# A list-scheduled transformer kernel: other queues and gates for the early stores, and products of constants ahead of the first weights

## The chip, the cores and the metric

The kernel runs on one core of a Trainium2 chip. The metric is the device time of one execution in microseconds (us). "TensorE" (PE in the profile; PEld is its weight load) multiplies matrices into eight banks of the accumulator memory; "VectorE" (DVE), "ScalarE" (ACT) and "GpSimd" (POOL) work on elements; "SyncE" (SP) here only issues transfers. SPq and ACTq in the profile are the queues on which SyncE and ScalarE issue transfers.

## The reference

Two blocks with residuals over 2048 tokens of 640 values. The first is attention over segments of 32 tokens; eight memory rows, which are outputs of the segment before, stand ahead of each segment, so the 64 segments depend on each other in a chain.

```python
x = A_x
h = x + _A_ref(_layernorm(x), A_mem0, A_Wq, A_Wk, A_Wv, A_Wo, A_seg_len)   # 32 heads of 128
h2 = h + _B_ref(_layernorm(h), B_W_gate, B_W_up, B_W_down)

# _A_ref, for each segment s of 32 tokens:
h = concatenate([mem, xs])                       # 8 memory rows + 32 tokens
q, k, v = h @ Wq, h @ Wk, h @ Wv
p = softmax(where(mask, q k^T * scale, -1e9))
o = (p v) @ Wo
mem = o[:8]; outs.append(o[8:])

# _B_ref:
h = (gate * (gate > 0)) * up                     # gate = x @ W_gate, up = x @ W_up, 1728 columns
return h @ W_down
```

## The kernel before

**Work.** A segment has 40 rows. 32 of them, the eight memory rows and the first 24 tokens, go through the chain of segments; the last eight tokens of each segment (the "rest") do not depend on the memory, so their query, key and value rows are made ahead for four segments at once. There are 16 such sets q of 128 rest rows, and each has six parts: query and key for either half of the heads (`p` = 0, 1) and values for either half (`p` = 2). A part is `groups`: five chunks of the contraction, each four products of 32 columns of rows by 512 columns of weights in one bank. `spread` evicts a query or key part, transposes it on VectorE into a staging tile `stg` (keys are reordered by GpSimd as well) and stores it to the scratch tensor `scr_qk` (line 1584); `values` evicts a value part into `stg` and stores it to `scr_v` (line 1601). `load_rs` brings the rest rows of one segment back into `RS`.

**The first 90 us.** The first nine sets (`EARLY = 9`) are made while the weights arrive: Wq, Wk and Wv in ten pieces each, then Wo in eight pieces of four heads. The rest rows of sets 0 to 3 and 4 to 7 come by `ln1r(0)` and `ln1r(1)`: a load of 128 rows (names "ldxr" and "ldxr1"), a layer norm on VectorE and ScalarE, a transpose by TensorE (20 products with the identity) and an eviction into `xr`. `ln1(0)` loads the first segments' rows ("ldx"). Rest rows of later sets are transposed by a transfer (line 1509). For sets 0 to 7 the names begin with "e": their `scr_qk` stores are issued by ScalarE, their `scr_v` stores by SyncE, and the latter wait until the fourth piece of Wo, `("Wo", 12)`, has landed. The early sets have up to eight banks and more staging tiles than later ones.

**A segment.** `main_qk` and `main_v` make query, key and value rows of the 32 rows; `scores` has the mask's seed, the products, an exponential on ScalarE, the sum by products with `bones`, logarithm and exponential for the reciprocal, and a product on VectorE; `pv` weights the values; `wo_early` and `wo` multiply by Wo (lines 1996 and 2015), `wo_add` adds the halves; `mem_next` copies the new memory rows into the next segment's input and transposes them (lines 1665 and 1668), which starts the next segment. Parts of rest sets, `rest_o` and the gate and up projections (`ahead`) are put into the segments as further work for TensorE. After the last segment come the weights of the second block and the down products.

**What sets the order.** All steps are declared by `op` with the engine, what they read and write, the buffers that they take, a cost and a transfer channel. `_Sched.schedule` then lists them once, in Python, with those costs: of the steps that are ready it takes the one with the highest level, which is the longest path to the end plus `BIAS[name]` and `BIAS["name@segment"]`. The result is a fixed order of instructions on each engine; at run time each engine works through its list and waits on semaphores. An eviction declared by `either` goes to ScalarE or VectorE, as `ENGINE` says, or else as the list comes out. `chan=(name, n)` allows n transfers of that name at a time. A transfer holds up whatever stands behind it in its engine's list until its inputs are there.

Two products of constants (`ones`, line 1866) fill banks 6 and 7 once at the start.

## Time and profile before

| | us |
|---|---|
| median of 3 runs | 998.73 (997.84 to 1000.79) |
| time of the profiled execution | 999.62 |
| span of the profiled execution | 997.5 |
| TensorE busy | 973.1 (98% of the span) |
| VectorE busy | 600.3 |
| ScalarE busy | 517.1 |
| GpSimd busy | 112.6 |

The span is measured from the first to the last instruction of the profile; the time of the execution is 2.1 us longer. The busy time of TensorE counts a matmul from its start to its modelled end, and matmuls overlap, so that it also holds time in which they run slowly. Rows of a group give its count, its busy time and the mean of one in ns, then the idle time just before them and what ended it.

### The profile page before, as it was taken

How to read it: one execution, taken by the hardware profiler on the slowest of the kernel's cores; microseconds unless marked ns; L12 is line 12 of the kernel's file. 1: busy time of each engine (PE TensorE's matmuls, PEld its weight loads, DVE VectorE, ACT ScalarE, POOL GpSimd, SP SyncE). 2: the span in 40 equal slices, each digit the busy share in tenths (PEclk: the TensorE clock that was granted, in tenths of full speed). 3: DMA queues.
4: the chain of work that ended last, by engine and by line, in shares of the span. 5: the costliest groups of instructions: out<-in, count | busy, mean ns of one | idle time of the engine just before them, and what ended most of it. 6: DMA issues, size and time to landing. Idle time of an engine off the chain costs nothing.

```text
span 997.5 us, 54364 instructions
## 1 busy us (share of the span) xinstructions
PE 973.1 (98%) x25380; PEld 528.0 (53%) x24412; DVE 600.3 (60%) x1307; ACT 517.1 (52%) x1264; POOL 112.6 (11%) x264
## 2 busy tenths in 40 slices
PE   6998999999999999999999999999999999999998
PEld 2344555555555555555565556555555556543343
DVE  5834666767675767566666676666665756523332
ACT  2245566566565565566555565556554665631020
POOL 3341011111011011001000010000100000100000
PEclk9999999999999999999999999999999999999999
DMA  9995121223131333232222343333233353289211
GB/s 334 407 334 137 44 57 55 68 67 76 35 90 40 85 74 79 53 80 65 72 77 61 86 105 85 86 88 78 55 79 82 76 92 85 53 270 288 76 40 40
DMA packets 181552, 103.60 MB, mean 104 GB/s; under 512 B 126212, under 2 KB 177484, under 8 KB 181324
## 3 DMA queue, kind: packets, MB, share of 16 engines
q1 hardware_dynamic: 175948, 95.51, 34.4%
q10 hardware_dynamic: 5376, 4.63, 1.4%
q8 instruction: 195, 3.19, 1.3%
q14 instruction: 33, 0.27, 0.1%
HBM read 67.30 MB, written 29.75 MB: 97 GB/s over the span
## 4 chain that ended last, share of the span: by engine, by line
PE 87%; SPq 3%; DMA 1%; ACTq 1%; ACT 1%; DVE 1%; issue 1%; POOL 0%; DVEq 0%
PE ps L1554 47%; PE ps L1996 7%; PE ps L2015 7%; PE ps L1719 7%; PE ps L1811 4%; PE ps L1638 3%; PE ps L1755 3%; PE ps L1962 3%; PE ps L1532 2%; PE ps L1937 2%; PE ps L1923 1%; SPq L2133 1%; ACTq L1598 1%; DMA scr_o<-osr 1%; SPq L1792 1%; SPq L2149 1%
## 5 line engine op out<-in xcount | busy, mean ns | idle before, releaser
L1388 ACT ACTIVATE tok<-ps 128x512 bf16<-128x512 f32 x225 | 133.4, 597 | 124.0 <-PE ps L1554 116.8
L1554 PE MATMUL ps<-Wk,xT 128*32 128x512 bf16 x2560 | 180.7, 379 | 0.6 <-ACT tok L1388 0.4
L1554 PE MATMUL ps<-Wv,xT 128*32 128x512 bf16 x2560 | 176.3, 379 | 0.0
L1554 PE MATMUL ps<-Wq,xT 128*32 128x512 bf16 x2560 | 169.3, 379 | 0.5 <-DVE xT L1668 0.3
L2045 DVE STREAM_TRANSPOSE QT<-tok 128x512 bf16<-128x512 bf16 x128 | 90.5, 708 | 50.7 <-ACT tok L1388 48.7
L2045 DVE STREAM_TRANSPOSE KT<-tok 128x512 bf16<-128x512 bf16 x128 | 90.8, 709 | 32.6 <-ACT tok L1388 31.4
L1554 PEld LDWEIGHTS ps<-Wq,xT 128*32 128x32 bf16 x2560 | 69.1, 97 | 68.4 <-DVE xT L1668 9.0
L1554 PEld LDWEIGHTS ps<-Wk,xT 128*32 128x32 bf16 x2560 | 65.9, 96 | 56.4 <-DVE xT L1668 3.9
L1932 ACT ACTIVATE E<-ps 128x224 bf16<-128x224 f32 x128 | 45.7, 357 | 91.6 <-PE ps L1927 88.0
L1389 DVE CAST oT<-ps 128x320 bf16<-128x320 f32 x128 | 56.8, 485 | 47.8 <-PE ps L1967 38.7
L2015 PE MATMUL ps<-Wo,oT 128*32 128x160 bf16 x4096 | 83.2, 233 | 0.3
L2015 PEld LDWEIGHTS ps<-Wo,oT 128*32 128x32 bf16 x4096 | 74.5, 97 | 14.5 <-ACT oT L1388 3.6
L1996 PE MATMUL ps<-Wo,oT 128*32 128x320 bf16 x2048 | 81.2, 300 | 0.8 <-ACT Vm L1388 0.6
L1554 PEld LDWEIGHTS ps<-Wv,xT 128*32 128x32 bf16 x2560 | 60.7, 96 | 38.4 <-DVE tok L1389 0.4
L1909 POOL COPY QT<-RS 128x256 bf16<-128x256 bf16 x64 | 25.8, 403 | 472.0 <-PE ps L1927 471.8
L1388 ACT ACTIVATE Vm<-ps 128x512 bf16<-128x512 f32 x121 | 71.5, 591 | 11.9 <-PE ps L1554 6.5
L1665 DVE CAST_PREDICATED xm<-turn,ps 128x64 bf16<-128x64 uint16 x126 | 28.0, 222 | 69.5 <-PE ps L1532 69.4
L1389 DVE CAST tok<-ps 128x512 bf16<-128x512 f32 x95 | 62.5, 658 | 9.9 <-PE ps L1554 9.8
L1996 PEld LDWEIGHTS ps<-Wo,oT 128*32 128x32 bf16 x2048 | 52.7, 96 | 27.7 <-DVE oT L1389 8.1
L1980 POOL COPY oTr<-oT 128x128 bf16<-128x128 bf16 x128 | 41.1, 321 | 198.6 <-ACT oT L1388 109.3
L1388 ACT ACTIVATE ps<-seed 128x384 f32<-128x384 bf16 x128 | 59.2, 489 | 1.4 <-DVE half L2004 1.3
L2004 DVE TENSOR_TENSOR half<-ps,half 128x320 bf16<-128x320 f32 x64 | 31.5, 492 | 42.2 <-ACT half L1388 41.8
(102 smaller groups left out, 1456.1 us busy)
## 6 DMA issues: line engine op xcount, KB each, us to landing
RS<-scr_qk SPq DMA_DIRECT2D x63, 128.0 KB, 2.3
big<-in_A_x_dram SPq DMA_DIRECT2D x34, 160.0 KB, 2.7
Wq<-in_A_Wq_dram SPq DMA_DIRECT2D x10, 512.0 KB, 7.1
Wk<-in_A_Wk_dram SPq DMA_DIRECT2D x10, 512.0 KB, 8.7
Wv<-in_A_Wv_dram SPq DMA_DIRECT2D x10, 512.0 KB, 7.7
Wo<-in_A_Wo_dram SPq DMA_DIRECT2D x8, 640.0 KB, 11.1
Wgs<-in_B_W_gate_dram SPq DMA_DIRECT2D x30, 160.0 KB, 3.0
Wus<-in_B_W_up_dram SPq DMA_DIRECT2D x30, 160.0 KB, 2.9
```

The source lines that it names most:

```text
L1388: return e.activation(dst, src, ACTF.Copy)
L1389: return e.tensor_copy(dst, src)
L1554: o = pe.matmul(out, lhs[c], rhs, start=(c == 0), stop=(c == DC - 1), skip_group_check=True)
L1638: o = pe.matmul(bank(bk)[p0:p0 + 32, 0:2 * SLICE], oTr[b][:, h, :], cols(h, 2 * a, 2 * a + 2), start=(h < 2), stop=(h >= H - 2), skip_grou ...
L1719: o = pe.matmul(bank(bk)[32 * i:32 * i + 32, 0:512], wt[:, c, 32 * i:32 * i + 32], xn2T[0][:, :, c * 128:(c + 1) * 128], start=(c == 0), s ...
L1811: pe.matmul(bank(ba)[:, 0:512], lhs, Wd[:, j, 0:512], start=(j == 0), stop=(j == FC - 1), skip_group_check=True)
L1932: op("act", lambda a: a.activation(E[:, g, :, 0:56], sco(BS[g]), ACTF.Exp, scale=SCALE), r=["table"], w=[("E", g)], x=[BS[g]], dur=0.36, n ...
L1980: op("pool", lambda e: e.tensor_copy(oTr[ob][:, 16 * g:16 * g + 16, XR * y:XR * y + XR], oT[:, 16 * g:16 * g + 16, 0:XR]), r=[("oT", g, 0) ...
L1996: o = pe.matmul(bank(BA)[p0:p0 + 32, 0:2 * SLICE], oT[:, h, XR:40], cols(h, 2 * b2, 2 * b2 + 2), start=(i == 0 and jj < 2), stop=(i == 3 a ...
L2004: op("dve", lambda v: v.tensor_tensor(half[1][:, :], bank(BA)[:, 0:2 * SLICE], half[0][:, :], ALU.subtract), r=["half0"], w=["half1"], x=[ ...
L2015: o = pe.matmul(bank(BW)[32 * j:32 * j + 32, 0:SLICE], oT[:, 16 + 4 * jj + i, XR:40], cols(h, j, j + 1), start=(i == 0 and jj == 0), stop= ...
L2045: op("dve", lambda v, tb=tb, dst=dst: v.transpose(dst, tok[tb.at][:, :].rearrange("p (h r) -> p h r", r=32)), w=[("QT" if p == 0 else "KT" ...
```

## The change

- `spread`: the four `scr_qk` stores of set 7 are issued by SyncE, on a channel of its own for six transfers; those of sets 0 to 6 stay with ScalarE.
- `values`: the `scr_v` stores of sets 0 to 7 wait for the second piece of Wo, `("Wo", 4)`, instead of the fourth.
- `norm1`: the load of the second rest rows ("ldxr1") is issued by SyncE. ScalarE keeps "ldx".
- `ln1r`: both evictions into `xr` are put on VectorE.
- `warm`: a new step of 44 products of the identity with the zeroed tile `E` into bank 6, which nothing reads. It needs the identity and `E`, as `ones` does.
- `BIAS` and `ENGINE`: of 3,596 entries of `BIAS`, 3,240 get another value, 353 go and 346 are new, over all segments. `ENGINE` has 466 entries instead of 361: 260 are new, 155 go, 29 change. With them the order on every engine, and which engine does an eviction, is listed anew for the whole kernel.

```diff
+WARM = 11
...
-BIAS = {"sel2": -489.03, "ezero": 890.66, "ldxs0": 802.72, "ldxs1": -1081.38, "ldxa": 905.72, "ldxl": -487.82,
...
-        op("act" if nm in ("ldx", "ldxr1") else "sp", lambda e: e.dma_start(big[xt.at][:, :], src), r=go, x=[xt], dur=0.6, lat=2.0,
-           chan=("xa" if nm in ("ldx", "ldxr1") else "x", 3), name=nm, xfer=0.5)
+        op("act" if nm == "ldx" else "sp", lambda e: e.dma_start(big[xt.at][:, :], src), r=go, x=[xt], dur=0.6, lat=2.0,
+           chan=("xa" if nm == "ldx" else "x", 3), name=nm, xfer=0.5)
...
+        ENGINE["ldxre"] = ENGINE["ldxr1e"] = "dve"
...
-            op("act" if early else "sp", lambda e: e.dma_start(
+            op("act" if early and q < 7 else "sp", lambda e: e.dma_start(
                 scr_qk[q, 2 * p + g, :, :], stg[t2.at][:, :]), w=[("scr_qk", q, p, g)], x=[t2], dur=0.4,
-               lat=2.2, chan=("rqe", 12) if early else ("rq", 4), name=early + "rdma", xfer=0.35)
+               lat=2.2, chan=("rqe", 12) if early and q < 7 else ("rqs", 6) if early else ("rq", 4), name=early + "rdma", xfer=0.35)
...
-               w=[("scr_v", q, g)], r=[("Wo", 12)] if early else [], x=[tb], dur=0.55, lat=2.2,
+               w=[("scr_v", q, g)], r=[("Wo", 4)] if early else [], x=[tb], dur=0.55, lat=2.2,
...
+    def warm(pe):
+        o = None
+        for k in range(WARM):
+            for j in range(4):
+                o = pe.matmul(ps[32 * j:32 * j + 32, 3072:3584], ident[:, 32 * j:32 * j + 32],
+                              E[:, :, :, :].rearrange("p g i c -> p (g i c)")[:, 0:512], start=True, stop=True, skip_group_check=True)
+        return o
+
+    op("pe", warm, r=["ident", ("E", 0), ("E", 1)], x=[banks(6)], dur=0.43 * WARM, n=8 * WARM, name="warm")
```

More of the change, by code (lines that the diff above doesn't have):

```diff
@@ L26 @@
 FPIECES = ((512, 896), (896, 1664), (0, 512))
[L27 to L28 removed]
[18 rows of a table removed]
[L47 to L48 removed]
[625 rows of a table removed]
[L674 to L677 removed]
[66 rows of a table removed]
+BIAS = {"sel2": -691.08, "ezero": 810.62, "ldxs0": 1235.79, "ldxs1": -1478.05, "ldxa": 655.43, "ldxl": -550.69,
+    "ldxx": 319.29, "ldxn": -1.84, "ldxx0": -313.85, "ldxst": -1532.78, "ldxxm": -560.22, "ldmev": -305.93,
[18 rows of a table added]
+    "gx": -82.78, "gxrelu": -879.5, "gxev": -232.87, "gxst": -288.9, "ln2nd": -1035.53, "xnld": 764.35,
+    "gld": 91.12, "gu": -0.76, "relu": 1559.66, "gmul": -918.54, "roz": -56.07, "tn2go": -266.85,
[620 rows of a table added]
+ENGINE = {"ldmev": "dve", "er0ev": "dve", "er0Tev": "act", "er1ev": "act", "ervev": "act", "r0Tev": "act",
+    "r1ev": "dve", "rvev": "dve", "Q0ev": "act", "Q0Tev": "act", "K0Tev": "act", "V0ev": "act", "Q1ev": "dve",
+    "Q1Tev": "dve", "K1ev": "act", "K1Tev": "act", "seed0": "act", "seed1": "act", "oTev0": "dve",
+    "oTev1": "act", "osrev": "act", "gxrelu": "dve", "er1ev@-1": "act", "K1ev@1": "act", "seed0@1": "act",
[85 rows of a table added]
 class _Slot:
```

7 lines of the change are left out of this document (removed), and 1432 rows, old and new, of tables (BIAS, ENGINE).

## The prediction

> **What bounds the kernel now.** I read the page's busy times and its chain first, then busy time by stretch, then the order of time wherever TensorE stands still.
>
> ```profile
> span 997.5 us, 54364 instructions
> PE 973.1 (98%) x25380; PEld 528.0 (53%) x24412; DVE 600.3 (60%) x1307; ACT 517.1 (52%) x1264; POOL 112.6 (11%) x264
> PE 87%; SPq 3%; DMA 1%; ACTq 1%; ACT 1%; DVE 1%; issue 1%; POOL 0%; DVEq 0%
> 5.00:10.00 5.00, 1.23 (x28) 0.70 (x32) 3.43 (x9) 2.73 (x8) 3.73 (x15) 1.00 1.03 391
> 60.00:70.00 10.00, 8.96 (x168) 4.01 (x156) 1.12 (x4) 1.68 (x3) 3.74 (x4) 1.00 1.08 359
> 70.00:80.00 10.00, 7.11 (x128) 3.02 (x124) 2.38 (x6) 5.98 (x16) 0.00 (x0) 1.00 0.67 174
> 80.00:90.00 10.00, 8.78 (x243) 4.46 (x235) 5.03 (x12) 5.43 (x14) 0.40 (x1) 0.83 0.60 145
> 300.00:400.00 100.00, 99.67 (x2955) 57.09 (x2863) 67.70 (x151) 59.79 (x149) 11.68 (x27) 1.00 0.29 70
> ```
>
> TensorE is the bound: 24.4 us of the span are without a matmul, and the chain is 87% its own. The stretch rows give length, then busy time of PE, PEld, DVE, ACT and POOL, clock, DMA share and GB/s. From 300 to 400 only 0.33 us is open; between 60 and 90 it is 1.04 + 2.89 + 1.22 = 5.15 us. The clock fell to 0.83 there as well, and matmuls at a lower clock count as busy. Until 70 us the DMA engines are full. So the named edits act on the first 90 us, where TensorE has the early sets' products to fill with; what they save comes off the end only if the 64 segments behind keep their pace.
>
> **The start.** The order of time (start, length, what, idle time before it):
>
> ```profile
> 0.82 1.36 ACTq L1480 DMA_DIRECT2D big<-in_A_x_dram  x2
> 2.62 1.04 PE L1866 MATMUL ps<-E,ident 128*32 128x512 bf16 x8 [2.62 <-POOL ident L1420]
> 7.96 0.72 PE L1518 MATMUL ps<-ident,big 128*32 128x128 bf16 x20 [4.30 <-DVE big L1474]
> 8.74 0.70 ACT L1388 ACTIVATE xr<-ps 128x640 bf16<-128x640 bf16 x1 [0.76 <-PE ps L1518]
> 9.49 4.50 PE L1554 MATMUL ps<-Wq,xr 128*32 128x512 bf16 x52 [0.81 <-ACT xr L1388]
> 9.89 0.16 PEld L1554 LDWEIGHTS ps<-Wq,xr 128*32 128x32 bf16 x4 [0.27 <-issue]
> 14.10 10.10 PE L1554 MATMUL ps<-Wq,xr 128*32 128x512 bf16 x184
> 14.32 0.49 DVE L1389 COPY xr<-ps 128x640 bf16<-128x640 bf16 x1 [1.65 <-PE ps L1518]
> ```
>
> The first 52 products take 4.50 us; at the pace of the next 184 (10.10/184 = 0.055 us each) they would take 2.85. The 1.65 us between is the slow clock after the idle start. `warm` adds 44 products into bank 6. At the pace of the eight constants' products (1.04/8 = 0.13 us) they take 5.7 us from 3.66, to 9.4. At the slow pace of the weight loads (0.16 + 0.27 = 0.43 us for four, 0.1075 each) they take 4.7, to 8.4. If the clock rises on the way as it did here, after 1.65/(0.1075 - 0.055) = 31 slow products, the constants' eight and 23 of warm's are slow and 21 fast: 3.6 us, to 7.3. The transposes could start at 7.96, so warm costs nothing (its cover is the 4.30 us wait) up to 1.4 us, and I take 0.2. The gain is 1.65 if the clock stays up, nothing if not; I take 1.65 less 0.2 = 1.45. No weights hold TensorE here: it keeps 0.055 us per product right through.
>
> Forcing xr's eviction to VectorE saves 0.70 - 0.49 = 0.21 us ahead of the first product (down to 0 if VectorE is at its statistics then). The second rest load moves from ScalarE's queue to SyncE's, ahead of the weights; two loads on ScalarE's queue took 1.36 us there, so one delays the weight stream by about 0.7 us at most, and TensorE runs behind that stream after 14 us. I cost it at nothing; uncovered it is 0.7.
>
> [...]
>
> **The stores.** What stands around the waits of 60 to 90 us:
>
> ```profile
> 49.65 11.08 SPq L1839 DMA_DIRECT2D Wo<-in_A_Wo_dram  x8
> 66.44 3.66 ACTq L1584 DMA_DIRECT2D scr_qk<-stg  x5
> 70.15 0.36 ACT L1932 ACTIVATE E<-ps 128x224 bf16<-128x224 f32 x1 [3.53 <-issue]
> 70.56 0.25 PE L1937 MATMUL ps<-E,bones 128*32 128x160 bf16 x4 [1.60 <-ACT E L1932]
> 71.24 1.05 PE L1554 MATMUL ps<-Wv,xr 128*32 128x512 bf16 x16 [0.40 <-ACT lnS L1945]
> 71.44 1.34 SPq L1509 DMA_TRANSPOSE xr<-big  x1
> 73.55 4.29 SPq L1601 DMA_DIRECT2D scr_v<-stg  x5
> 77.80 2.56 ACT L1388 ACTIVATE stg<-ps 128x512 bf16<-128x512 f32 x5 [3.37 <-DMA scr_v<-stg]
> 78.94 1.26 PE L1554 MATMUL ps<-Wq,xr 128*32 128x512 bf16 x20 [1.83 <-ACT stg L1388]
> 81.00 1.90 PE L1554 MATMUL ps<-Wq,xr 128*32 128x512 bf16 x16 [0.80 <-DVE tok L1389]
> 85.43 1.27 PE L1996 MATMUL ps<-Wo,oT 128*32 128x320 bf16 x32 [0.27 <-DVE oT L1389]
> 87.75 1.28 PE L2015 MATMUL ps<-Wo,oT 128*32 128x160 bf16 x64
> SPq L1509 <- DVE stat L1462: 7.0, 1, 7.0
> 81.00:82.00 1.00, 1.00 (x12) 0.47 (x16) 0.69 (x1) 0.00 (x0) 0.00 (x0) 0.50 0.87 204
> 82.00:83.00 1.00, 1.00 (x36) 0.46 (x24) 0.00 (x0) 0.00 (x0) 0.00 (x0) 0.50 0.71 160
> 83.00:84.00 1.00, 0.89 (x21) 0.11 (x4) 0.44 (x1) 0.86 (x3) 0.40 (x1) 0.50 0.38 85
> ```
>
> ScalarE issues stores from 66.44 to 70.15 with the first exponential behind them, and TensorE loses 1.60 + 0.40 = 2.00 us to that chain. Set 7's four stores leave this queue: at 3.66/5 = 0.73 us each that is 2.9 us of issue, more than the 2.00, so I take all of it (nothing, if the four stood before 66 us with slack behind them). On SyncE's queue they cost the same issue time, and whoever stands behind them waits if a transposed row is not ready.
>
> SyncE issues no values' store before 73.55. Then staging buffers are short: ScalarE's eviction waits 3.37 us for a store to land, TensorE 1.83 and then 0.80 us. After these gaps the clock shows 0.50 for three microseconds; 2.89 us busy at half speed is 1.45 us lost. Together 1.83 + 0.80 + 1.45 = 4.08. The gate on the second piece of Wo instead of the fourth opens earlier by two of eight issues, 11.08/8 x 2 = 2.8 us, and puts stores into SyncE's 7.0 us stand before the transposing load. That is more than the 1.83 us wait, so I take all 4.08 (nothing, if SyncE's head of queue decides; see the rivals).
>
> What is late next is Wo itself, since stores now land between its pieces.
>
> ```profile
> DMA to landing us min/median/max: 7.2/11.1/11.7
> scr_v<-stg SPq DMA_DIRECT2D x32, 128.0 KB, 2.7
> 74.00:76.00 2.00, 2.00 (x44) 0.98 (x40) 0.61 (x1) 0.40 (x3) 0.00 (x0) 1.00 0.87 188
> ```
>
> The last piece was issued by 60.7 (49.65 + 11.08) and lands by 72.4. Stores alone moved 188 GB/s at a share of 0.87, so 216 at full share; 128 KB is 0.61 us. Sixteen of them ahead of the last piece put it at 72.4 + 9.8 = 82.2; eight at 77.3. Without the losses above the second half's products (87.75) would come at 87.75 - 1.45 - 0.21 - 2.00 - 4.08 = 80.0. Sixteen cost 2.2 us, eight nothing; as most sets have values by then, I take 2.0.
>
> Sum: -1.45 - 0.21 - 2.00 - 4.08 + 2.0 = -5.7 us. The tables give almost every step another priority and many evictions another engine; the page has 0.33 us open in 100, while work that overlaps less can hide inside busy time, so I put 0 with 3 us either way. The profiled execution took 999.62 us, 2.1 beyond its span and 0.9 above the median of the three runs, 998.73: 999.62 - 5.7 = 993.9 by its own time, 993.0 from the median. I say 993.5.
>
> **The rivals.**
>
> *SyncE's queue only changes place.* The row of the 7.0 us wait says SyncE stood at the transposing load of the rest rows, which needed ScalarE; Wo's fourth piece, issued near 54, had landed by about 66, long before 73.55. If the stores stay behind that load, or set 7's stores stop the queue, the stores' 6.1 us do not come and only the start's 1.66 does: 998.0 by the own time, 997.1 by the median. For it: SyncE is one line of order. Against: ScalarE's freed issue time moves that load too.
>
> *The warm clock is lost over the transposes.* Then 1.65 us go: 995.5, or 994.7 by the median. For it: 77 to 81 us, where gaps of 1.83 and 0.80 us sufficed to bring 0.50. Against: the gaps at the start are shorter in all.
>
> *Slower: the segments lose their cover.* Each segment hands its memory rows from TensorE through VectorE back to TensorE:
>
> ```profile
> L1665 DVE CAST_PREDICATED xm<-turn,ps 128x64 bf16<-128x64 uint16 x126 | 28.0, 222 | 69.5 <-PE ps L1532 69.4
> ```
>
> At two copies a segment, the 126 stand for 63 hand-overs. TensorE fills this time with rest and gate products. If the new order puts fewer there, a hand-over is exposed; the start's gain is used up at 5.7/63 = 0.09 us each. An exposure of 0.15, below one copy's 0.222, gives 63 x 0.15 - 5.7 = +3.8: 1003.4. For it: nearly all priorities differ, over 800 us. Against: the hand-overs' chain kept within 0.33 us open per 100 us, and no resource of a segment is changed.
>
> **How the numbers follow.** Forecast 0.47, SyncE's queue 0.20, lost clock 0.10, slower 0.18; 0.05 for segments that also gain 5 us, about 988. About 0.3%, 3.0 us, is what a measurement of this kernel can tell from no change: 995.7 and 1001.7 are the bounds. Nearly all of the forecast, most of the lost clock and a little of the queue's case lie below 995.7, with the 0.05: faster 0.60. The queue's case is most of same: 0.20. Slower: 0.20. The range runs from 988.5 (forecast with 3 us from the segments and Wo on time) to 1003 (just short of the slower case).
>
> **What would show it.** Right: the first Wq products at 0.055 us each; the first exponential not behind issues of ScalarE; values' stores from about 62 us; no 0.50 clock near 81; the first L1996-type product with Wo near 79; stretches after 100 us as full as before. Wrong: that product at 84 or later (SyncE's queue or Wo), half pace after the transposes, or a first such product early with segments that take longer than before.

## The result, and the profile after

The changed kernel took 1003.43 us (median of 22 runs, 998.9 to 1006.61); the kernel before took 1000.33 us beside it (22 runs, 997.84 to 1003.98). The ratio is 1.0027, with a 95% interval of 1.0018 to 1.0037: slower by about 0.3%, where 993.5 us was forecast. Of the 9.9 us between the forecast and the result, some 1.2 lie in its base: it started from 998.73 (median of three runs) and 999.62 (the profiled execution). The profiled execution of the changed kernel took 1002.14 us, 2.5 more than that of before (999.62).

The page's span, busy times and chain:

```profile
span 1000.3 us, 54467 instructions
PE 978.7 (98%) x25434; PEld 538.2 (54%) x24456; DVE 624.6 (62%) x1349; ACT 496.3 (50%) x1222; POOL 112.7 (11%) x264
PE 90%; DMA 5%; SPq 2%; DVE 1%; issue 1%; ACT 1%; POOL 1%; ACTq 0%; DVEq 0%; POOLq 0%
```

TensorE is the bound as before, and DMA has grown from 1% to 5% of the chain. Busy time by stretch of the changed kernel (length, then PE, PEld, DVE, ACT, POOL, clock, DMA share, GB/s):

```profile
10.00:15.00 5.00, 4.12 (x60) 1.75 (x60) 1.37 (x6) 0.94 (x4) 0.00 (x0) 0.66 1.03 414
60.00:70.00 10.00, 9.12 (x172) 4.18 (x164) 1.31 (x5) 3.02 (x8) 3.61 (x4) 1.00 1.08 361
70.00:80.00 10.00, 7.87 (x140) 3.15 (x128) 2.02 (x5) 4.34 (x10) 0.00 (x0) 1.00 0.99 217
80.00:90.00 10.00, 8.91 (x272) 4.82 (x264) 7.72 (x17) 6.09 (x15) 2.57 (x3) 1.00 0.57 134
300.00:400.00 100.00, 99.67 (x2967) 60.41 (x2864) 68.30 (x153) 57.26 (x143) 11.99 (x28) 1.00 0.27 72
```

From 300 to 400 us TensorE is as full as before. From 60 to 90 us 4.10 us are open instead of 5.15, and the half clock near 81 is gone; but a half clock now stands in the first 15 us, and 70 to 80 us is DMA at a share of 0.99 where before had 0.67. The order of time on TensorE at the start:

```profile
3.44 4.82 PE L1891 MATMUL ps<-E,ident 128*32 128x512 bf16 x44
9.14 0.40 PE L1570 MATMUL ps<-Wq,xr 128*32 128x512 bf16 x4 [0.60 <-DVE xr L1404]
9.80 0.40 PE L1570 MATMUL ps<-Wq,xr 128*32 128x512 bf16 x4 [0.27 <-DMA Wq<-in_A_Wq_dram]
11.09 3.73 PE L1570 MATMUL ps<-Wq,xr 128*32 128x512 bf16 x36 [0.89 <-DMA Wq<-in_A_Wq_dram]
```

The constants' products end at 8.26, and the clock is released at 8.03 us by the trace's clock record (12.59 in the kernel before; the stretch rows read 1.00 ahead of the first record, so they do not show the slow start). TensorE then waits 0.27 and 0.89 us for pieces of Wq, and the clock falls again from 11.44 to 14.86: 36 products take 0.104 us each. Then 62 to 85 us, over SyncE's queue, ScalarE and TensorE:

```profile
64.38 2.04 SPq L1600 DMA_DIRECT2D scr_qk<-stg  x2
68.55 0.36 ACT L1958 ACTIVATE E<-ps 128x224 bf16<-128x224 f32 x1 [1.85 <-issue]
69.83 1.34 SPq L1524 DMA_TRANSPOSE xr<-big  x1
71.71 0.60 ACT L1403 ACTIVATE stg<-ps 128x512 bf16<-128x512 f32 x1 [1.75 <-DMA scr_qk<-stg]
71.98 2.89 SPq L1617 DMA_DIRECT2D scr_v<-stg  x4
72.36 0.83 PE L1570 MATMUL ps<-Wv,xr 128*32 128x512 bf16 x12 [1.46 <-ACT stg L1403]
73.56 0.83 PE L1570 MATMUL ps<-Wv,xr 128*32 128x512 bf16 x12 [0.37 <-ACT stg L1403]
84.85 1.26 PE L2022 MATMUL ps<-Wo,oT 128*32 128x320 bf16 x32
```

The first exponential comes at 68.55 instead of 70.15, and the transposing load and the values' stores behind it 1.6 us earlier than before. In their place ScalarE waits 1.75 us for a `scr_qk` store to land, and TensorE 1.46, 0.37 and 0.30 us for ScalarE. The first product with Wo comes at 84.85 (85.43 before), not near 79.

VectorE's transposes of the new memory rows (`xT<-xm`) mark the hand-overs from one segment to the next. Shown are the first, with which the second segment starts, and the last, with which the last segment starts. Before:

```profile
89.46 0.24 DVE L1668 STREAM_TRANSPOSE xT<-xm 128x64 bf16<-128x64 bf16 x1
866.21 0.24 DVE L1668 STREAM_TRANSPOSE xT<-xm 128x64 bf16<-128x64 bf16 x1
```

After:

```profile
88.87 0.25 DVE L1684 STREAM_TRANSPOSE xT<-xm 128x64 bf16<-128x64 bf16 x1
865.89 0.24 DVE L1684 STREAM_TRANSPOSE xT<-xm 128x64 bf16<-128x64 bf16 x1
```

So the changed kernel is 0.59 us ahead at the first hand-over, 0.32 ahead at the last, and 2.8 behind at the end (131.3 us of tail before, 134.4 after; "tail" is the time from the last hand-over on). The groups of the tail that changed, before (from 866.2 us on):

```profile
L1811 PE MATMUL ps<-Wd,gT 128*128 128x512 bf16 x94 | 26.3, 379 | 0.8 <-DVE osr L1647 0.8
L1638 PE MATMUL ps<-Wo,oTr 128*32 128x320 bf16 x128 | 5.1, 300 | 0.0
L1719 PE MATMUL ps<-xn2T,Wus 128*32 128x512 bf16 x8 | 0.6, 379 | 0.0
L1719 PE MATMUL ps<-xn2T,Wgs 128*32 128x512 bf16 x4 | 0.4, 379 | 0.0
```

After (from 865.9 us on):

```profile
L1827 PE MATMUL ps<-Wd,gT 128*128 128x512 bf16 x98 | 27.1, 379 | 2.5 <-ACT osf L1403 1.5 <-DVE osr L1663 1.0
L1654 PE MATMUL ps<-Wo,oTr 128*32 128x320 bf16 x120 | 4.8, 300 | 0.0
L1735 PE MATMUL ps<-xn2T,Wus 128*32 128x512 bf16 x20 | 1.4, 381 | 0.0
L1735 PE MATMUL ps<-xn2T,Wgs 128*32 128x512 bf16 x20 | 1.4, 379 | 0.0
```

The new order leaves gate and up products to the tail that stood in the segments before (2.8 us busy instead of 1.0), and the down products wait 2.5 us instead of 0.8. (Both kernels have the same down products; some of their records are missing from the profile of before, hence 94 and 98.) A wait of 1.3 to 2.0 us for ScalarE's eviction into `osf` stands in this place in the changed kernel and in `a_xact`, `a_nowarm`, `a_wolate` and `a_tail` below, and not in the kernel before or `b_again`.

### The profile page after: what moved, and what is told of

The parts are those of the page before. It is cut to its first block, busy times and chain, and to the rows that moved or that the text cites. A ratio compares the mean times of both kernels' runs of the same rounds, so it can differ in the third digit from the quotient of the medians.

```text
span 1000.3 us, 54467 instructions
## 1 busy us (share of the span) xinstructions
PE 978.7 (98%) x25434; PEld 538.2 (54%) x24456; DVE 624.6 (62%) x1349; ACT 496.3 (50%) x1222; POOL 112.7 (11%) x264
## 4 chain that ended last, share of the span: by engine, by line
PE 90%; DMA 5%; SPq 2%; DVE 1%; issue 1%; ACT 1%; POOL 1%; ACTq 0%; DVEq 0%; POOLq 0%
PE ps L1570 48%; PE ps L2022 7%; PE ps L2041 7%; PE ps L1735 7%; PE ps L1827 4%; PE ps L1771 4%; PE ps L1654 3%; PE ps L1988 3%; DMA scr_qk<-stg 2%; PE ps L1548 2%; PE ps L1963 2%; PE ps L1949 1%; DMA Wu<-in_B_W_up_dram 1%; DMA Wq<-in_A_Wq_dram 1%; DMA scr_o<-osr 1%
## 5 line engine op out<-in xcount | busy, mean ns | idle before, releaser
L1403 ACT ACTIVATE tok<-ps 128x512 bf16<-128x512 f32 x209 | 124.1, 597 | 153.5 <-PE ps L1570 141.3
L1570 PE MATMUL ps<-Wq,xT 128*32 128x512 bf16 x2560 | 171.8, 379 | 1.5 <-DVE xT L1684 1.5
L1570 PEld LDWEIGHTS ps<-Wq,xT 128*32 128x32 bf16 x2560 | 71.3, 96 | 66.2 <-DVE xT L1684 11.8
L1570 PEld LDWEIGHTS ps<-Wk,xT 128*32 128x32 bf16 x2560 | 70.4, 96 | 55.1 <-issue 1.4
L1404 DVE CAST tok<-ps 128x512 bf16<-128x512 f32 x111 | 73.3, 661 | 12.4 <-PE ps L1570 12.1
L1403 ACT ACTIVATE ps<-seed 128x384 f32<-128x384 bf16 x122 | 56.2, 489 | 5.9 <-DVE half L2030 4.5
```

The costliest lines, as they stand in the source:

```text
L1403: return e.activation(dst, src, ACTF.Copy)
L1404: return e.tensor_copy(dst, src)
L1570: o = pe.matmul(out, lhs[c], rhs, start=(c == 0), stop=(c == DC - 1), skip_group_check=True)
```

## The experiments

In each the planner's list is taken as it was for the kernel named and only the lines shown are changed in it; nothing else is listed anew. A row's line number is that of the experiment's own file. "Before" in a ratio is the kernel before on the same chip; the equal kernel's run shows how far two equal kernels come apart.

### The edits without the tables, and each alone

`b_edits`, in the kernel before:

```diff
+ TensorE:  ones, ones, warm (44 products)
- ScalarE:  ldxr1 ... four stores of set 7     xr's eviction
+ SyncE:    ldxr, ldxr1 ... four stores of set 7
+ VectorE:  xr's eviction
- values' store waits for ("Wo", 12)
+ values' store waits for ("Wo", 4)
```

> The kernel before with every edit of the code (constants' products, both token loads on SyncE's queue, VectorE's eviction of the transposed rest rows, set 7's four stores on SyncE's queue, the values' gate on the fourth Wo piece), and with the order of every other instruction kept as in the kernel before: only the new tables of the planner are left out. Theory A (the edits save little, because the first Wq pieces land 1.5 us later and set 7's stores land behind Wo; what the changed kernel loses, it loses in the end and in the segments that the tables reordered): 998 to 1000 us where before has 1000.3, the first segment's transposes about 0.6 us earlier than before and the stretch behind the last segment's start still 131.3 us long. Theory B (the sum of the prediction holds for the edits and the tables alone took it back): 994 to 995.5 us. Theory C (the edits themselves are what costs): 1002 to 1004 us.

(The gate meant is that on `("Wo", 4)`, the second piece.) 1001.87 us, ratio 1.0011 (0.9999 to 1.0024). Theory B is out by far; the result lies between A and C: the edits bring nothing, and perhaps cost a little. The first hand-over at 88.89 was 0.57 us earlier than in the kernel before, as A had it; `b_again` below came 1.44 earlier with no edit, so this is within the spread. Here the clock stayed up behind the constants' products, and still the lead went:

```profile
9.42 3.01 PE L1637 MATMUL ps<-Wq,xr 128*32 128x512 bf16 x52 [0.60 <-DVE xr L1472]
23.83 4.72 PE L1637 MATMUL ps<-Wq,xr 128*32 128x512 bf16 x84 [0.57 <-DVE tok L1472]
32.55 1.26 PE L1637 MATMUL ps<-Wk,xT 128*32 128x512 bf16 x20 [1.68 <-DVE tok L1472]
73.53 6.13 PE L1637 MATMUL ps<-Wv,xr 128*32 128x512 bf16 x80 [2.63 <-ACT stg L1471]
```

The first 52 products took 3.01 us instead of 4.50, as predicted. Then TensorE waited for evictions, 3.5 us in all between 20 and 62 us against 2.3 in the kernel before, and at 73.53 for ScalarE, whose buffers had not been stored.

`b_warm`, in the kernel before:

```diff
+ TensorE:  ones, ones, warm (44 products)
```

> The kernel before with the 44 constants' products put behind its two first ones and nothing else changed. Prediction: the clock is released near 8 us, the first 52 Wq products run at full pace and all that follows comes 1.45 us earlier: 998.8 us. Rival: the products at full pace overtake the weights, TensorE stands in waits for Wq pieces, and the clock falls again behind them as in the changed kernel (0.50 from 11.4 to 14.9 us): no gain, 1000.0 to 1000.6 us. If the 44 products slow the weights' transfers, the second Wq piece lands near 9.8 us as in the changed kernel; if not, near 8.2 us as in the kernel before.

1002.41 us, ratio 1.0016 (1.0001 to 1.0031): not faster, rather slower. The clock was released at 7.0 us and did not fall before 71.9 us. The first hand-over came at 89.47, as in the kernel before, so a gain of 1.45 us is excluded. Of the rival's mechanism half came true: TensorE waited 1.34 us for Wq, but the clock did not fall behind it. The second Wq piece landed at 9.40. One part of the price was not foreseen; it stands in the last section.

`a_nowarm`, in the changed kernel:

```diff
- TensorE:  ones, ones, warm (44 products)
+ TensorE:  ones, ones
```

> The changed kernel without the 44 constants' products, nothing else changed. Prediction's sum: 1.45 us slower than the changed kernel, 1004.9 us. Theory D (the DMA engines are full from 8 to 72 us in every kernel, so time won before them is lost again where VectorE and ScalarE wait for staging buffers whose stores have not landed): the clock is released near 12 us, yet the first segment's transposes start within 0.5 us of the changed kernel's, and the time is 1002.5 to 1003.9 us. Rival (the products themselves cost, by the transfers or by more windows at half clock, as the 1.7 us of the kernel before with them suggest): 1001.2 to 1002.2 us.

1002.44 us, ratio 1.0011 (0.9997 to 1.0026) where the changed kernel has 1.0027. The result lies between D and the rival. In both orders the ratio is 0.0016 higher with the products; the interval of `b_warm` just leaves out 1, the two of the changed order overlap. So the size is open, but a gain of 1.45 us is not there. In this profile the first hand-over came at 91.39, 2.5 us later than in the changed kernel, where D had allowed 0.5; as `b_again` shows, one such pair settles little.

`b_q7`, in the kernel before:

```diff
- ScalarE:  four stores of set 7
+ SyncE:    four stores of set 7
```

> The kernel before with set 7's four stores of queries and keys issued on SyncE's queue, at the same place of the order, and nothing else changed. Prediction's term: TensorE's two waits for ScalarE at 70.56 and 71.24 (1.60 and 0.40 us) go: 998.3 us. Rival: the stores land behind the eight Wo pieces whichever queue issues them, so the values' evictions that wait for their buffers come as late as in the changed kernel (ScalarE 1.75 us, TensorE 1.46 us at 72.4), and at most 0.5 us is left: 999.8 to 1000.5 us.

1001.37 us, ratio 1.0005 (0.999 to 1.002): the predicted 2.0 us less lie outside the interval. TensorE's wait at the exponential's sum fell from 1.60 to 0.57 us, and a new one stands behind it:

```profile
70.60 0.25 PE L1993 MATMUL ps<-E,bones 128*32 128x160 bf16 x4 [0.57 <-ACT E L1988]
75.59 6.74 PE L1610 MATMUL ps<-Wv,xr 128*32 128x512 bf16 x72 [3.05 <-ACT stg L1444]
```

Set 7's last two stores, issued at 64.04 and 65.81 behind Wo's pieces on SyncE's queue, landed after 9.9 and 8.8 us; the first two had gone out at 48.83 and 51.81. ScalarE's wait behind the 3.05 us ended at 74.94, with the landing of a store of its own, issued at 68.04. In this run the weights were late from the start (the second Wq piece landed at 10.78), so the 3.05 is not all the edit's.

`a_xact`, in the changed kernel:

```diff
- SyncE:    ldxr, ldxr1, Wq pieces ...
+ SyncE:    ldxr, Wq pieces ...
+ ScalarE:  ldx, ldxr1
```

> The changed kernel with the second rest load of tokens on ScalarE's queue again, behind the first block's load, and nothing else changed. Theory (this load, put on SyncE's queue between the first load and the first Wq piece, is what makes the pieces land 1.5 us later): the second Wq piece lands near 8.3 us instead of 9.8, TensorE's waits for Wq go, the clock stays released from 8 us on, and the whole comes 2 to 3 us earlier: 1000.4 to 1001.4 us where the changed kernel has 1003.4. Rival (the 44 products or the chip make the transfers slow, not the queue): the second piece lands near 9.8 us again and the time stays within 0.5 us of 1003.4.

1003.74 us, ratio 1.0029 (1.0016 to 1.0043): no difference, and the second Wq piece landed at 9.76 us as in the changed kernel. The theory fell. The moved load, now behind that of the memory rows, landed at 9.94 and held VectorE, so that the first Wq product waited 3.57 us; TensorE then found its weights there, and the clock stayed up.

`b_again` is the kernel before, unchanged.

> The kernel before once more, unchanged, for a second profile and for what the comparison gives two equal kernels. Both theories: ratio 1.000 with 1 in its interval. Theory N (a profile differs from the next one of the same kernel by gaps of TensorE in which nothing is waited for, and by the number and place of the 3.41 us windows at half clock): this profile has sums of such gaps that differ from the first one's 0.33 us by about 1 us or more, and its segment starts drift against the first profile's by steps of 0.4 to 0.9 us with the same order of instructions. Theory P (such steps are made by the edits): the two profiles keep within 0.3 us of each other from the second segment on.

999.92 us, ratio 0.999 (0.9975 to 1.0004). Its first hand-over came at 88.02, 1.44 us earlier than in the first profile, with the same instructions; this lead stayed the same to within 0.3 us up to the 18th segment, then drifted in steps of 0.3 to 0.7 us to 2.7 and back to 1.45 at the last. TensorE's gaps of over 0.3 us with nothing waited for summed up to 1.31 us (0.33 in the first). So theory N holds, and single profiles are read here only for mechanisms and for differences that several of them share.

### Whether the weights' bytes bound the start

`b_w3` and, with 2 in place of 3, `b_w2`, in the kernel before:

```diff
- chan=("w", 5)    # pieces of Wq, Wk, Wv in flight
- chan=("wo", 8)
- SyncE:  ... Wo 0..7, ln1
+ chan=("w", 3)
+ chan=("wo", 2)
+ SyncE:  ... Wo 0..5, ln1, Wo 6, Wo 7
```

> The kernel before with three of the weight pieces (Wq, Wk, Wv) in flight at a time instead of five, and two Wo pieces instead of eight (the last two issued behind the next block's load); nothing else changed. Theory D (a staging buffer's store lands behind all the weight bytes in flight, 6 to 8 us after its issue between 16 and 60 us against 2.2 us at 83 us, and VectorE, ScalarE and then TensorE wait for those buffers): the stores land in 4 to 5 us, TensorE's 2.6 us of waits for VectorE's rows between 20 and 60 us and 1.8 us for staging buffers near 73 us shrink, the first segment's transposes start 1.5 to 3 us earlier and the time is 998 to 999.3 us. Rival (the weights themselves are the bound, and fewer pieces in flight leave the DMA engines idle): the pieces land later one by one, TensorE waits for them, 1001.5 to 1004 us.

> As b_w3, with two weight pieces in flight. Theory D: the stores land in about 3 to 4 us; if the DMA engines stay full, the gain is that of b_w3 or 0.5 us more; if two pieces no longer cover the time from issue to landing, the pieces land each later than the last and it is slower than b_w3. Rival: 1004 to 1010 us, further than b_w3 in the same direction.

1013.12 us, ratio 1.0109 (1.0085 to 1.0134), and 1031.8 us, ratio 1.0275 (1.0248 to 1.0301). The rival was right, by more than it had said. A stretch of `b_w3` and then of the kernel before:

```profile
20.00:30.00 10.00, 10.00 (x192) 4.78 (x188) 7.19 (x14) 0.00 (x0) 0.29 (x1) 1.00 1.00 349
```

```profile
20.00:30.00 10.00, 8.96 (x168) 3.97 (x164) 6.45 (x13) 0.00 (x0) 0.29 (x1) 1.00 1.05 402
```

The rate fell from 402 to 349 GB/s. In `b_w3` the last Wv piece landed 11.7 us later than before (64.5 for 52.8) and the first hand-over came 14.7 us later (104.11); in `b_w2` it came at 119.72. TensorE's waits for weight pieces sum up to 7.0 us in `b_w3`, where the kernel before has none. The edit also makes Wo later, with its last piece at 88.5 instead of 70.4, and a wait of 5.74 us for a staging buffer stands at 92.52; how much of the 14.7 is due to which was not separated.

`b_w3warm` is `b_w3` with warm as in `b_warm`, `a_w3` the edit of `b_w3` in the changed kernel.

> As b_w3, with the 44 constants' products as well. Theory D (what the released clock wins before 14 us was lost to late stores only): with the stores landing early the 1.45 us of the prediction are kept, 1 to 1.5 us under b_w3, 996.8 to 998.2 us. Rival (the products cost as much as they bring, by later weights or windows at half clock): within 0.5 us of b_w3, or above it as the kernel before with them was above the kernel before.

> The changed kernel with the edit of b_w3, nothing else. Theory D: set 7's stores land in 3 to 4 us instead of 7, TensorE's waits for staging buffers of 1.46, 0.37 and 0.30 us behind 72 us go, and the time is 1.5 to 3 us under the changed kernel, 1000.5 to 1002 us. Rival: as slow as the changed kernel or slower, 1003.4 to 1006 us.

1016.78 us, ratio 1.0138 (1.0114 to 1.0161), and 1017.13 us, ratio 1.0143 (1.0118 to 1.0169). The products did not pay here either, and the changed kernel keeps its distance from the kernel before (0.34% here).

`b_w8`, in the kernel before:

```diff
- chan=("w", 5)
+ chan=("w", 8)
```

> The kernel before with eight pieces of Wq, Wk and Wv in flight instead of five, nothing else changed. Theory D1 (with five the DMA engines already move all they can, 377 to 411 GB/s): the pieces land no earlier one by one, the stores land 2 to 4 us later than before, 1001 to 1003.5 us. Theory D2 (what bounds the rate is the number of pieces in flight, as 294 to 350 GB/s with three suggests, and five are still too few): the last Wv piece lands 1 us or more before 52.8 us and the time is 998 to 1000 us.

999.64 us, ratio 1.0005 (0.9992 to 1.0018): no difference. The last Wv piece landed at 52.96 us (52.80 before), so with five pieces the weights already come as fast as with eight, as D1 says; but the stores issued between 16 and 60 us took 7.0 us in the middle, as before (6.9), and D1's loss didn't come.

### What holds 62 to 85 us

`a_wolate`, in the changed kernel:

```diff
- SyncE:  ... Wo 4..7, ln1, store, store (set 7), ln1rT
+ SyncE:  ... ln1, store, store (set 7), Wo 4..7, ln1rT
```

> The changed kernel with the last four of the eight Wo pieces (2.6 MB) issued behind set 7's last stores instead of ahead of the next block's load, nothing else changed. Theory D (the stores that ScalarE and TensorE wait for at 71 to 76 us land late because Wo's transfers stand ahead of them): set 7's stores land 2 to 3 us after their issue instead of 7, TensorE's 1.46, 0.37 and 0.30 us of waits for staging buffers behind 72 us go, no half clock behind them, and the time is 1 to 2.5 us less, 1001 to 1002.4 us. Rival (the stores wait for their own chain on GpSimd and the transposing load, not for Wo): the waits stay, and Wo's last piece, now landing near 76 us, changes nothing before the first Wo product at 84.85: 1003.0 to 1003.8 us; if that product comes later than 84.9, slower.

1005.74 us, ratio 1.004 (1.0026 to 1.0054): slower. Set 7's two stores ahead of the pieces did land 2.5 us after their issue. ScalarE's stores issued beside the pieces from 65.39 on then took 6.4 to 7.5 us, and TensorE waited 4.1 us for ScalarE instead of 2.6. So here the pieces delayed whatever was issued behind or beside them, and moved later they delayed other stores.

`b_wospread`, in the kernel before:

```diff
- SyncE:  ... Wo 4..7, ln1, ln1rT, values' stores
+ SyncE:  ... ln1, ln1rT, Wo 4, two stores, Wo 5, two stores, Wo 6, store, Wo 7 ...
```

> The kernel before with the last four Wo pieces issued one by one behind the transposing load and behind the first values' stores on SyncE's queue, from about 71 to 79 us, nothing else changed. Theory D (2.6 MB less ahead of the stores of 65 to 70 us; behind 72 us the DMA engines are only half full): the stores land in 2 to 3 us, the values' stores go out earlier, each with one piece ahead of it at most, the last piece lands before the products of the second half of heads need it at 87.75 us, and the time is 1 to 2.5 us less, 998.3 to 999.8 us. Rival (as with four pieces behind set 7's stores, what comes behind the pieces is late in its turn, the values' stores here): 1001 to 1004 us.

1007.03 us, ratio 1.0072 (1.0052 to 1.0092). The stores of 65 to 69 us landed in 1.8 to 2.3 us, the values' stores behind the pieces in 4 to 6 us: the rival's mechanism, at more than its price.

`b_halfwo`, in the kernel before:

```diff
- SyncE:   load Wo 4..7
+ GpSimd:  memset(Wo 4..7, 0)
```

> The kernel before with the last four Wo pieces (2.6 MB) not loaded but filled with zeros by GpSimd between 10 and 20 us, where it stands idle: heads 16 to 31 contribute nothing to the output projection. Nothing else is changed. Theory D (up to 72 us the bytes are the bound, and what ScalarE's stores and the values' stores wait for is the transfers ahead of them): the DMA engines run empty near 63 us, the stores issued at 65 to 70 us land in 2 to 3 us instead of 5, TensorE's idle time from 65 to 85 us shrinks by 2 to 3 us and the time is 997.5 to 999 us where before has 1000.8. Rival (those waits hang on the chain of evictions, GpSimd's copies and the transposing load, not on bytes): 1000 to 1001.3 us.

1002.39 us, ratio 1.0027 (1.0015 to 1.004). This run doesn't tell the theories apart. The fill ran from 19.6 to 28.7 us, not by 20, held GpSimd's copies and made the start late. The stores landed in 1.7 to 1.9 us, and TensorE still stood 4.3 us in waits between 72 and 89 us, 1.68 of it for ScalarE's evictions behind the values' stores. So fewer bytes alone did not close this stretch.

`b_exp`, in the kernel before; `a_exptail` is the same edit in the changed kernel (and nothing at the tail, despite its name), `b_editsexp` the same in `b_edits`:

```diff
  ScalarE:  ... ldrs x4
+           exp0, two instructions of the rest rows' norm
            evictions of set 1, store issues
-           exp0, two instructions of the rest rows' norm
```

(The recorded texts count sets from one here; set 1 is their set 2.)

> The kernel before with three short instructions of ScalarE moved ahead in its queue, nothing else changed: the first exponential (0.36 us, at 70.15) and the two of the rest rows' normalisation (0.28 and 0.20 us) go ahead of set 2's evictions and the seven store issues that wait for GpSimd's last copy at 65.5, since their inputs are there near 61 us. Theory C (the chain: GpSimd's copies, ScalarE's store issues, first exponential and normalisation, VectorE's row that waited 9.8 us for them, the transposing load at 71.44, the values' stores behind it at 73.55, the evictions that wait for those): the transposing load goes near 67.5 us, the values' stores near 70 us, TensorE's waits of 1.60 and 0.40 us at 70.56 and 71.24 and most of 1.83 us at 78.94 and 0.8 us behind it go, 2 to 4 us less: 996 to 998.5 us where before has 1000. Rival D (the DMA engines, full until Wo's last piece at 70.4 us, hold what is issued earlier): the values' stores land no earlier than 76 us, 0 to 0.8 us less, 999.2 to 1000.5 us.

> The kernel before with all edits of the code and the move of b_exp, the order of all else kept. Theory C (the edits left the chain as it was, and once it is cut they have nothing more to give): within 1.2 us of b_exp to either side. Prediction's terms (clock 1.45 us, ScalarE's freed queue 2.0 us, gate 4.1 us): 2 us or more under b_exp, below 996 us.

> The changed kernel with the same three instructions of ScalarE moved ahead of set 2's evictions and of the six store issues before the first exponential, nothing else changed. Theory C: the exponential runs near 66 instead of 68.55 us, the transposing load near 68 instead of 69.83, and 1 to 2.5 us go: 1001 to 1002.5 us where the changed kernel has 1003.4. Rival D: set 7's stores and the evictions behind them at 71.7 stay as they are, within 0.6 us of 1003.4.

`b_exp`: 1000.14 us, ratio 0.9988 (0.9974 to 1.0003); no better than what the equal kernel showed. `b_editsexp`: 1005.03 us, 1.0035 (1.002 to 1.005). `a_exptail`: 1008.04 us, 1.0052 (1.0034 to 1.0069). The move did what it should: the exponential ran at 66.38, 66.04 and 65.56, the transposing load at 67.67, 67.33 and 66.84. But with the edits it made the kernel slower. Theory C had the issues right and not the landings: in `b_exp` the transposing load went out 3.77 us earlier than in the kernel before and landed 0.13 us earlier, at 74.06, which is rival D's mechanism. The interval reaches into the ranges of both. Transfers issued from 66 to 79 us, with their median time to landing, and the DMA engines' busy tenths and rate over the same time in 40 slices; before:

```profile
DMA  9999999999999999762019920599989584006979
GB/s 307 362 358 357 408 326 342 349 357 342 334 367 349 365 354 328 258 230 79 25 27 211 217 53 10 131 245 195 195 173 251 114 219 91 11 18 138 218 161 225
scr_qk<-stg ACTq DMA_DIRECT2D x6, 128.0 KB, 4.9
xr<-big SPq DMA_TRANSPOSE x1, 2.8
```

The changed kernel with the move (`a_exptail`):

```profile
DMA  9999999999999999979964699900399999999953
GB/s 324 335 366 358 364 347 360 353 355 348 359 370 366 345 333 284 275 255 237 225 172 156 182 314 125 30 11 8 70 265 249 207 229 276 305 285 285 289 110 83
scr_qk<-stg ACTq DMA_DIRECT2D x6, 128.0 KB, 9.1
xr<-big SPq DMA_TRANSPOSE x1, 10.1
```

The changed kernel:

```profile
scr_qk<-stg ACTq DMA_DIRECT2D x5, 128.0 KB, 5.7
xr<-big SPq DMA_TRANSPOSE x1, 5.0
```

In the kernel before the transposing load goes out at 71.44, when Wo has landed and the stores are nearly through; it takes 2.8 us, the rate dips to 25 and 27 GB/s, and no store of this stretch is out for more than 5.4 us. Issued at 66.84 it stands in the middle of the early stores: the rate falls to 8 to 30 GB/s about 74.5 us while stores issued at 67 and 69 us are still out, and they land after 9.1 us. TensorE's wait for a staging buffer, first `b_exp`, then `a_exptail`:

```profile
74.64 4.50 PE L1617 MATMUL ps<-Wv,xr 128*32 128x512 bf16 x80 [1.72 <-ACT stg L1451]
```

```profile
76.05 1.47 PE L1633 MATMUL ps<-Wv,xr 128*32 128x512 bf16 x12 [4.65 <-ACT stg L1466]
```

It was 4.20 us in `b_editsexp`, 2.63 in `b_edits` and 1.46 in the changed kernel, and in the kernel before it stands later, with 1.83 us at 78.94. What `b_exp` lacks and the others have is set 7's stores on SyncE's own queue ahead of the transposing load, and the early lead; which of them makes the wait longer was not tried. In `b_warm`, with the queues of before, the wait already stands at 72.91 with 1.82 us.

### The tail

`a_tail`, in the changed kernel:

```diff
- SyncE:  ... gate rows' load (5.01 us of issue), store, store (rest rows of the last set)
+ SyncE:  ... store, store (rest rows of the last set), gate rows' load
```

> The changed kernel with one load of the gate rows (the one that took 5.01 us of SyncE's queue at 905.07) issued behind the two stores of the last segment's rest rows instead of ahead of them, nothing else changed. Theory T (these stores, issued 5 us late, hold VectorE's next addition at 916.48 and TensorE 1.02 us at 917.02): the stores go out near 906 us, that wait goes and the time is 0.5 to 1 us less, 1002.4 to 1002.9 us. Rival (the end is set by the products of the feed-forward that the tables moved behind the last segment, and the wait is refilled by the next one): within 0.3 us of the changed kernel, 1003.1 to 1003.7 us.

1002.68 us, ratio 1.0011 (0.9997 to 1.0026). The median agrees with theory T, the interval doesn't exclude the rival, and the profile speaks for the rival: its tail is 134.2 us long, that of the changed kernel 134.4. TensorE's wait behind these stores fell from 1.02 to 0.53 us, and the one for `osf` ahead of it grew from 1.48 to 1.80. The one move tried here leaves the tail as long as it was. Time of the first hand-over ("start"), from there to the last one ("segments") and from there to the end of the span ("tail"), from each kernel's profile (us):

| order of before | start | segments | tail | order of the changed kernel | start | segments | tail |
|---|---|---|---|---|---|---|---|
| before | 89.5 | 776.8 | 131.3 | changed | 88.9 | 777.0 | 134.4 |
| b_again | 88.0 | 776.7 | 132.3 | a_xact | 90.2 | 774.5 | 134.7 |
| b_q7 | 92.0 | 778.4 | 131.9 | a_nowarm | 91.4 | 775.2 | 135.6 |
| b_w8 | 88.8 | 776.5 | 131.5 | a_wolate | 91.6 | 774.3 | 134.3 |
| b_exp | 88.4 | 777.8 | 131.8 | a_tail | 88.1 | 775.2 | 134.2 |

The tails don't overlap: means of 131.75 and 134.63 us. The segments' means are 777.24 and 775.27. Kernels left out of the table bear the tails out: 131.5 to 131.8 in `b_halfwo`, `b_wospread`, `b_w3` and `b_w2`, 134.8 and 134.9 in `a_exptail` and `a_w3`. (`b_edits`, `b_warm`, `b_editsexp` and `b_w3warm` stand apart with 132.7 to 134.7; their tails hold the stall of the last section.) They do not bear the segments out: with them the two orders overlap, 775.5 to 778.6 and 774.3 to 779.8. So the tables put 2.9 us into the tail; that they take 2.0 out of the segments is not shown. No run has the tables without the edits.

## Why the prediction was wrong, by its steps

The step that failed with most at stake is the stores' 6.08 us (2.00 and 4.08): the time of TensorE without a matmul between 60 and 90 us fell from 5.15 to 4.10 us, by 1.05, since the `scr_qk` stores of this stretch were issued earlier (from 64.38 instead of 65.60) and landed no earlier (the last at 74.02 instead of 72.90). The tables, put at 0, cost 2.9 us in the tail, which in the profiled executions outweighs what was won.

**The start (-1.45 - 0.21).** The mechanism was right: warm ends at 8.26 (7.3 to 9.4 were worked out), the clock is released 4.6 us earlier, and in `b_edits` the 52 products took 3.01 us for the predicted 2.85; xr's eviction fell to VectorE's 0.49 us. The step that failed is "no weights hold TensorE here". It was read from one profile, in which the second piece of Wq had landed at 8.21 us, and that was luck. In kernels that leave the start as it was, without the 44 products, that piece landed at 8.04 (`b_again`), 8.20 (`b_w8`), 9.74 (`b_wospread`), 10.26 (`b_exp`), 10.78 (`b_q7`) and 11.11 us (`b_halfwo`), and in the last four TensorE waited 1.2 to 2.8 us for Wq although it ran at the slow clock. `b_exp`:

```profile
8.91 0.62 PE L1617 MATMUL ps<-Wq,xr 128*32 128x512 bf16 x4 [1.36 <-DMA Wq<-in_A_Wq_dram]
```

With the products it was 1.16 us in the changed kernel, 1.34 in `b_warm` and 0.32 in `b_edits`, and what `b_edits` won there went in longer waits for evictions. So the landing of the weights, which differs by up to 3 us from one execution to the next, can hold the start with either clock. The rows that pointed there, DMA shares of 1.03 from 5 to 10 us and 1.08 from 60 to 70, were quoted and not used. `b_w3` and `b_w2` agree (less in flight, later start, though Wo was later too). In place of -1.45 the products brought nothing by the first hand-over (`b_warm`: 89.47 for 89.46) and no gain in the end.

**The lost clock (a rival).** It fell in the changed kernel, after waits of 0.60, 0.27 and 0.89 us, and also within 7 us of its release in `a_wolate` and `b_editsexp`. In `b_edits`, `b_warm` and `a_xact` the same constants' products and transposes came first and the clock stayed up to 71.9 us or more. So the transposes did not cost the clock in these three runs. What cost it in the others is open: `b_warm` had waits of 0.82, 0.20 and 1.14 us, more than the changed kernel, and `a_xact` one of 3.57.

**ScalarE's queue (-2.00).** 1.60 us did go at the exponential. Behind it TensorE now waits 1.46, 0.37 and 0.30 us from 72 us on: ScalarE's evictions come earlier, and their buffers do not. The stores of this stretch land behind Wo, at 70.9 to 72.9 us in the kernel before and at 71.0 to 74.0 in the changed one. ScalarE's three waits end at 71.71, 72.91 and 74.04 us. Set 7's store of 64.38 landed at 71.71, after 7.3 us, and ScalarE's own stores of 67.54 and 68.03 at 72.89 and 74.02; in `b_edits` and `b_q7` the long wait ends with a store of ScalarE's own. The error was to price the move by issue time alone and not by where the stores land. The term was too large even so: only two of set 7's four stores stood in the stretch that it was read from (in `b_q7` they go out at 64.04 and 65.81, the other two by 51.81), which makes 1.5 us of issue and not 2.9.

**The values' gate (-4.08).** The rival "SyncE's queue only changes place" was right in its mechanism. The next block's load, ahead on SyncE's queue and unchanged, still waits for the fourth piece, and the transposing load stands between; the first values' store came at 71.98, 1.57 earlier, not near 62. That was the transposing load's gain. The wait of 1.83 us for a staging buffer became the 2.13 us at 72 to 75, that of 0.80 became 0.49 and 0.34, and the half clock there was missing in this profile; in `b_edits` and `a_xact` it came, some 7 us earlier. Its 1.45 us were thus saved by luck of the execution: `b_again`, the kernel before once more, has no half clock there either.

**Wo later (+2.0).** Nothing: the last piece landed at 70.25 (70.40 before), as no values' store went out between the pieces. **The second rest load (0):** not contradicted; `a_xact` shows no difference in time, though there the load came late.

**The tables (0, with 3 either way).** The stretch from 300 to 400 us is as full as forecast, and the hand-overs of the slower rival were not exposed. The loss sits where no step of the prediction looked, from the last hand-over on: +2.9 there, against -2.0 in the segments by the table's means, which the other kernels do not confirm.

The start brings about -0.6 in the profiled executions and is within the spread of equal kernels; the tables bring +0.9 by the table's means and +1.9 with the kernels left out of it; the rest of the 2.7 is not settled by rows. A part goes with the clock: the mean granted clock was 0.9975 over the changed kernel's 22 runs and 0.9984 over 35 runs of the kernel before beside the first experiments (0.9985 to 0.9993 beside the others), and 0.0009 of 1000 us is 0.9 us. Among the 22 runs the four at a clock of 1.0 took 1000.8 us on average, the five at 0.995 took 1004.9. No kernel here is shown to beat the kernel before.

## What to carry to other kernels

Here, with the DMA engines at a share of 1.08 from 60 to 70 us, an earlier issue alone was worth little (in `b_exp` the transposing load went out 3.77 us earlier and landed 0.13 earlier): price a moved store by issue to landing in that stretch (7.3 us for the one of 64.38), not by its issue (0.34 us). What stands in one profile may be absent from the next one of the same kernel (the half clock of 3.41 us near 81 us in the first profile of the kernel before, and none there in `b_again`), so read a second profile before a term rests on it. Before pricing a gate, look for an older wait ahead of it in the same queue. And when an order is listed anew, compare the stretch behind the last loop as well as the loop: here gate and up products left the loop and arrived behind it (1.0 us busy there before, 2.8 after).

## What the runs showed that was not expected

**A stall at a fixed place of TensorE's instructions.** `b_warm` lost 1.71 us near 880 us with nothing waited for, `b_edits`, `b_editsexp` and `b_w3warm` 1.42 to 1.44 at the same product; `b_again`, `b_q7`, `b_exp` and `b_halfwo`, without the 44 products, 0.35 to 0.36, a little further on. `b_warm` and then `b_q7`:

```profile
878.10 0.24 PE L2035 MATMUL ps<-E,Vm 32*128 32x40 bf16 x11
880.06 0.21 PE L2035 MATMUL ps<-E,Vm 32*128 32x40 bf16 x5 [1.71 <-issue]
```

```profile
879.63 0.27 PE L2018 MATMUL ps<-E,Vm 32*128 32x40 bf16 x16
879.74 0.19 PE L2023 MATMUL ps<-E,RS 32*128 32x64 bf16 x4
879.87 0.73 PE L1694 MATMUL ps<-Wo,oTr 128*32 128x320 bf16 x16
880.57 0.53 PE L2071 MATMUL ps<-Wo,oT 128*32 128x160 bf16 x19
881.46 0.74 PE L2071 MATMUL ps<-Wo,oT 128*32 128x160 bf16 x32 [0.36 <-issue]
```

From the 11th of the 16 `E,Vm` products to the gap of `b_q7` it is 5 + 4 + 16 + 19 = 44 products: exactly those added 870 us earlier. The gap keeps its place in the count of instructions, ahead of product 24,556 or 24,557 in all eight, and the added ones moved it to where it costs 1.1 to 1.4 us more. In `b_warm`'s profile 3.41 us at half clock follow from 880.82 on. The place is one of a grid: in the 20 profiles, all 59 such gaps over 0.28 us behind the first 100 us stand where the count of TensorE's products is 81 plus a whole multiple of 129.5, to within 5. Not every place has one in every execution (the first profile of the kernel before has none here). What makes it was not tried.

**The transposing load among other transfers.** With little else out it took 2.7 to 2.8 us from issue to landing (the kernel before, `b_halfwo`, `b_wospread`), among stores 3.5 to 10.1, and in `a_exptail` the rate fell to 8 to 30 GB/s for about a microsecond while others waited. The load moves 160 KB; a store of 128 KB took 2.2 us near 84 us. Whether the transposition or the queue ahead of it makes the difference was not tried.

**A store's time to landing.** 128 KB took 2.2 us from issue to landing near 84 us. Between 16 and 60 us the median was 6.9 us with five weight pieces of 512 KB in flight, 7.0 with eight, 5.4 with three and 4.9 with two. The issue itself took 0.32 to 0.88 us for the eight stores of 64 to 69 us in the changed kernel, and their buffers were gone for the 5.4 to 7.3 us to landing.
